# A two-problem attention decode: the framework's context closed behind the first six loads, the rest a bare program

## The chip, the cores and the metric

One core of one Trainium2 chip. The metric is device time in microseconds (us) of one execution, taken as the median of several runs. The engines are named as in the profile: PE is the matrix engine, DVE the vector engine, ACT the scalar engine, POOL is GpSimd, SP the engine that here only issues transfers. A "q" behind a name (SPq, ACTq) means the queue of that engine, on which transfers are issued.

## The reference: what is computed

Two attention layers decode one token each, A over a whole cache and B over its last 4096 positions. Both have 32 heads of width 128, each with its own keys and values, all bf16. The outputs of 512 each are set side by side.

```python
q = (x @ wq).reshape(1, 1, 32, 128)              # x: 1x1x512, wq: 512x4096
scores = einsum("bhqd,bhkd->bhqk", q, k) * 128 ** -0.5
p = softmax(scores)                              # A: 16384 keys a head; B: the last 4096
o = einsum("bhqk,bhkd->bhqd", p, v)
y = o.reshape(1, 1, 4096) @ wo                   # wo: 4096x512
# result: concatenate([yA, yB], axis=-1)
```

The caches that must be read are 32 x 16384 x 128 x 2 bytes x 2 for A and a quarter of it for B. With the weights that is 352 MB.

## The kernel before

**Stages.** The work is 20 steps of 8 MB of keys and 8 MB of values. Steps 0, 7, 13 and 19 are B steps (eight heads each), the other 16 are A steps (two heads each). Three 8 MB slots hold the data: `slotX` and `slotY` take the keys of even and odd steps, `slotV` takes the values of every step but the last, whose values go into `slotX`.

**One step.** DVE multiplies the keys by the query in place (L300, two halves), adds the 128 products of a key in a tree (L309, then the reduction of L316 into `sc`), and takes a maximum (L323). PE transposes the maxima (L389), DVE makes one maximum of a head and copies it to all partitions' places in `Mr` (L331, L335), PE transposes that back (L391), and ACT copies it times -1/sqrt(128) into `bias` (L347), takes the exponential (L352) and spreads the probabilities into `pm` (L360). PE multiplies them with the values in 64 small matmuls (L396) into `o`, ACT copies `o` to `osb` (L383), and PE folds it into the accumulators of A and B with two matmuls whose weights `fwA` and `fwB` choose the rows (L406). ACT writes the fold weights of a step at L376 or L379. Where step T-1 belongs to the other layer, ACT first clears the old weights (L374). There are six such places: T = 1, 7, 8, 13, 14, 19.

**What orders the work.** All waits are written by hand with counting semaphores. `_Lane.need` makes an engine wait for a token, `_Lane.did` makes one, and `_Loads.put` makes a token of a transfer. PE runs 19 of the 20 steps in a loop (L456) and takes tickets (L164). SP issues every load in program order: keys of step T+1 when DVE has reduced step T-1 (L316), values of step T when PE has used those of step T-1 (L396). POOL waits for the values of a step and passes this on to PE as a ticket (`to_v`, L431). In the last step SP issues the six loads of the two output weights `wo` (L441), once PE has used the values of step 18.

**Start.** ACT issues the two loads of x (L205). SP issues four loads of 4 MB: `wq` of B (L196), the first half of B's keys (L180), `wq` of A (L196), the second half (L180). Beside them POOL makes an identity (L213, L215) and clears `fwA`, `fwB` and part of `PA` (L220). DVE clears two buffers (L227), makes masks and patterns (L229 to L236), and, when PE has transposed x (L242), spreads it into block matrices (L246, L255). PE multiplies these with `wq` (L270), and ACT copies the queries (L276).

**End.** When the last piece of `wo` is there PE ends the output of B (L588), DVE copies it (L594), ACT and SP each store half (L598), and ACT waits for the stores (L602).

**The framework's part.** Buffers come from tile pools of a `TileContext` (opened at L628), and everything from L202 to L602 lies in one critical section of it (L201). The program that results has these parts around the hand-written one: after the start-up of L617 (four constants by POOL, one barrier over all engines) SP posts a semaphore at L201, on which all five engines wait and branch into the section; behind the section stand a chain of drains and semaphores that ends in one of SP (L201), and then a barrier, a clearing of the semaphores by POOL, and a second barrier (L628).

Of the kernel before, what the change touches and what calls it, by code (L numbers as in the profile page):

```python
# [8 lines left out]
F32 = mybir.dt.float32  # L9
BF16 = mybir.dt.bfloat16  # L10
P = 128
# [45 lines left out]
def kernel(  # L57
# [24 lines left out]
    low = ctx.enter_context(tc.tile_pool(name="low", bufs=1))  # L82
    slots = ctx.enter_context(tc.tile_pool(name="slots", bufs=1))
    high = ctx.enter_context(tc.tile_pool(name="high", bufs=1))
    banks = ctx.enter_context(tc.tile_pool(name="banks", bufs=1, space=bass.MemoryType.PSUM))

    def sbuf(pool, name, n, dt=F32, p=P):
        return pool.tile([p, n], dt, tag=name, name=name)

    def bank(name):  # L90
        return banks.tile([P, 512], F32, tag=name, name=name)

    qA = sbuf(low, "qA", HQ // 2 * DH, BF16)
    qB = sbuf(low, "qB", HQ // 4 * DH, BF16)
    identf = sbuf(low, "identf", P)
    fw = [sbuf(low, "fwA", P), sbuf(high, "fwB", P)]
    Mr = sbuf(low, "Mr", P, p=2)
    PB = sbuf(low, "PB", QR)
    PA = sbuf(low, "PA", 16)
    csA, csB = sbuf(low, "csA", HQ // 2), sbuf(low, "csB", HQ // 4)  # L100
    maskA, maskB = sbuf(low, "maskA", 2), sbuf(low, "maskB", 4)
    sbuf(low, "pad", 8)
    X, Y, W = (slots.tile([P, 2 * CH, DH], BF16, tag=n, name=n) for n in ("slotX", "slotY", "slotV"))
    pm = sbuf(high, "pm", 2 * CH // 4 * QR + QR, BF16)
    osb = sbuf(high, "osb", 512)
    sc = sbuf(high, "sc", 2 * CH)
    m, M, bias = sbuf(high, "m", 2), sbuf(high, "M", 4, p=2), sbuf(high, "bias", 2)
# [33 lines left out]
    for T in range(HQ // 2 + HQ // 8):  # L141
# [8 lines left out]

    pe, dve, act, pool, sp = (
        _Lane(e, tc.alloc_semaphore(n))
# [5 lines left out]
    in_x, in_wqB, in_wqA, in_v, in_out = (_Loads(tc.alloc_semaphore(n)) for n in ("in_x", "in_wqB", "in_wqA", "in_v", "in_out"))  # L158
    in_k = [[_Loads(tc.alloc_semaphore(f"in_k{a}{b}")) for b in range(2)] for a in range(2)]
    in_last = [_Loads(tc.alloc_semaphore(f"in_last{u}")) for u in range(2)]  # L160
    to_m, to_r, to_pm, to_v, to_f = (tc.alloc_semaphore(n) for n in ("to_m", "to_r", "to_pm", "to_v", "to_f"))
# [12 lines left out]
    def load(T, cache_a, cache_b, dst, loads, parts=(0, 1)):  # L174
        s, g = steps[T]
        if s is A:
            return [loads[0].put(nc.sync.dma_start(out=dst, in_=a_pair(cache_a, g)))]
        n = CH * DH
        return [
            loads[u].put(nc.sync.dma_start(out=dst[:, u * n : (u + 1) * n], in_=b_window(cache_b, 2 * g + u)))  # L180
            for u in parts
        ]
# [11 lines left out]
    def load_wq(s, dst, loads):  # L194
        return loads.put(
            nc.sync.dma_start(  # L196
                out=dst.rearrange("p (c f) -> p c f", c=KC), in_=s.wq.rearrange("(p c) f -> p c f", c=KC)
            )
        )

    with tc.tile_critical(no_gpsimd_drain=True):  # L201
        half = CH * DH  # L202
        xrow = pm[0:2, 0:D]
        for s in (B, A):
            x_in = in_x.put(nc.scalar.dma_start(out=xrow[s.k : s.k + 1, :], in_=s.x[0, :, :]))  # L205
        wq = [fW[:, half : 2 * half], fW[:, 0:half]]
        wq_in = [None, load_wq(B, wq[1], in_wqB)]
        load_k(0, (0,))
        wq_in[0] = load_wq(A, wq[0], in_wqA)
        load_k(0, (1,))  # L210


        t = pool.did(nc.gpsimd.memset(identf[:, :], 0.0))  # L213
        pool.need(t)
        ident = pool.did(nc.gpsimd.affine_select(  # L215
            out=identf[:, :], in_=identf[:, :], compare_op=ALU.not_equal, fill=1.0, base=0,
            pattern=[[-1, P]], channel_multiplier=1,
        ))
        for f in (fw[0][:, :], fw[1][:, :], PA[:, 0:8]):
            cleared = pool.did(nc.gpsimd.memset(f, 0.0))  # L220
        n = KC * P
        xb = [osb[:, :].bitcast(BF16)[:, 0 : 2 * n], fY[:, 0 : 4 * n]]
        two_b = fY[0:2, 8 * n : 8 * n + 2]
        xT = [fY[:, 8 * n + 64 * (k + 1) : 8 * n + 64 * (k + 1) + KC] for k in range(2)]
        for s in (B, A):
            s.xb = xb[s.k].rearrange("p (h c m) -> p h c m", h=s.nh, c=KC)
            dve.did(nc.vector.memset(xb[s.k], 0.0))  # L227
        dve.need(ident)
        two = dve.did(nc.vector.tensor_copy(two_b, identf[0:2, 0:2]))  # L229
        for s in (B, A):  # L230
            dve.did(nc.vector.tensor_reduce(out=s.mask[:, :], in_=by_head(s, identf[:, :]), axis=AX.X, op=ALU.add))
        t = dve.did(nc.vector.tensor_reduce(
            out=PB[:, :], in_=identf[:, :].rearrange("p (g x) -> p x g", g=NG), axis=AX.X, op=ALU.add
        ))
        dve.need(t)
        consts = dve.did(nc.vector.tensor_tensor(out=PA[:, 8:16], in0=PB[:, 0:8], in1=PB[:, 16:24], op=ALU.add))  # L236

        xps = wide[:, 0 : 2 * KC].rearrange("p (c s) -> p c s", s=2)
        pe.need(x_in, two)
        xr = xrow.rearrange("s (p c) -> s c p", c=KC)  # L240
        for c in range(KC):
            mm = nc.tensor.matmul(xps[:, c, :], lhsT=xr[:, c, :], rhs=two_b, start=True, stop=True)  # L242
        turned = pe.did(mm)
        dve.need(turned)
        for s in (B, A):
            t = dve.did(nc.vector.tensor_copy(xT[s.k], xps[:, :, s.k]))  # L246
        dve.need(t)
        for s in (B, A):
            for j in range(s.nh):
                dst = s.xb[:, j, :, :]  # L250
                if s is A:
                    dst = dst.rearrange("p c (h i) -> p c h i", h=s.nh)[:, :, j, :]
                else:
                    dst = dst.rearrange("p c (i h) -> p c i h", h=s.nh)[:, :, :, j]
                t = dve.did(nc.vector.tensor_copy(dst, xT[s.k].unsqueeze(2).broadcast_to([P, KC, P // s.nh])))  # L255
            s.spread = t
        pool.need(turned)
        zeroed = pool.did(nc.gpsimd.memset(pm[:, :], 0.0))

        qcopy = []  # L260
        for s in (B, A):
            pe.need(wq_in[s.k], s.spread)
            w = wq[s.k].rearrange("p (c g h d) -> p c h g d", c=KC, h=s.nh, d=DH)
            for g in range(0, HQ // s.nh, 4):
                qp = (t0, t1)[len(qcopy) % 2][:, :].rearrange("p (g d) -> p g d", d=DH)
                if len(qcopy) >= 2:
                    pe.need(qcopy[-2])
                for k in range(KC * s.nh):
                    c, j = divmod(k, s.nh)
                    mm = nc.tensor.matmul(  # L270
                        qp, lhsT=s.xb[:, j, c, :], rhs=w[:, c, j, g : g + 4, :],
                        start=(k == 0), stop=(k == KC * s.nh - 1),
                    )
                projected = pe.did(mm)
                act.need(projected)
                qcopy.append(act.did(nc.scalar.copy(s.q[:, g : g + 4, :], qp)))  # L276
                s.q_in = qcopy[-1]
            if s is B:
                freed_y = projected
                pe.need(zeroed)  # L280
                for a in (accA, accB):
                    mm = nc.tensor.matmul(
                        a[:, :], lhsT=pm[:, 0:P], rhs=pm[:, 0:512], start=True, stop=False, skip_group_check=True
                    )
                seeded = pe.did(mm)
        freed_w = projected
        loop0 = pe.n
        TR1, TR2, PV, FOLD = 1, 2, 3, 4

        def at(T, k):  # L290
            return (pe.sem, loop0 + 4 * T + k)
# [3 lines left out]
        def scores_prod(T, u):  # L295
            s, g = steps[T]
            kt = kflat(T)[:, u * half : (u + 1) * half].rearrange("p (l d) -> p l d", d=DH)
            j = g if s is A else 2 * g + u
            dve.need(kin[T][min(u, len(kin[T]) - 1)], s.q_in)
            return dve.did(nc.vector.tensor_tensor(  # L300
                out=kt, in0=kt, in1=s.q[:, j : j + 1, :].broadcast_to([P, CH, DH]), op=ALU.mult
            ))

        def scores_tree(T, lo, hi, t):
            k = kflat(T).rearrange("p (l d) -> p l d", d=DH)[:, lo:hi, :]
            w = DH // 2
# [7 lines left out]
            if T >= 1:  # L314
                dve.need(exped[T - 1])
# [317 lines left out]
```

## Time and profile before

| what | value |
|---|---|
| median of 3 runs | 822.28 us (822.17 to 822.59) |
| the profiled execution's own time | 822.12 us |
| its span, first to last instruction | 820.2 us |
| DVE busy | 755.9 us (92%) |
| PE busy | 193.7 us (24%) |
| ACT busy | 58.1 us (7%) |
| POOL busy | 2.9 us, 10 instructions |
| bytes read | 352.32 MB, 430 GB/s over the span |

Times inside the execution count from the span's first instruction. The profiled execution took 1.9 us more than its span, and 0.16 us less than the median. Drains, branches and semaphore instructions do not count as busy and have no row of their own on the page; the trace holds a start and a duration for each, and some of these are quoted by number.

### The profile page before, as it was taken

The numbers are of one execution on the slowest core, as the hardware profiler recorded it, in microseconds if no ns is written. First come the engines' busy times: TensorE is split into PE (matmuls) and PEld (weight loads), VectorE is DVE, ScalarE is ACT, GpSimd is POOL, SyncE is SP. The second block draws the span as 40 slices with busy tenths as digits, with TensorE's granted clock in tenths as the row PEclk, the third lists the DMA queues.
The fourth block names the chain that finished last, engine by engine and source line by source line (L and its number), as shares of the span: only waits on it lengthen the run. The fifth ranks groups of instructions, "written<-read, shape, count | busy, mean of one in ns | idle before, by whom it ended". The sixth has DMA issues, their size and how long they took to land. (4 is left out here: it accounts for less than half of the span.)

```text
span 820.2 us, 4069 instructions
## 1 busy us (share of the span) xinstructions
PE 193.7 (24%) x1638; PEld 78.4 (10%) x1638; DVE 755.9 (92%) x264; ACT 58.1 (7%) x171; POOL 2.9 (0%) x10
## 2 busy tenths in 40 slices
PE   3500312223030403030403122130304030304036
PEld 1200100101010101010101001010101010101012
DVE  2899999999999999899999999998999999999992
ACT  0101000001010000100000000010100000000010
POOL 1000000000000000000000000000000000000000
PEclk9865656565665656565656565655656565656568
DMA  9999999999999999999999999999999999999997
GB/s 384 435 434 436 457 412 454 416 454 416 454 416 451 411 449 428 420 446 431 438 422 447 422 447 414 455 413 431 438 454 416 454 416 454 416 431 438 431 435 312
DMA packets 8084, 352.40 MB, mean 430 GB/s; under 512 B 907, under 2 KB 1038, under 8 KB 1294
## 3 DMA queue, kind: packets, MB, share of 16 engines
q1 hardware_dynamic: 8068, 352.33, 99.3%
q8 instruction: 3, 0.05, 0.0%
q14 instruction: 3, 0.02, 0.0%
q10 hardware_dynamic: 10, 0.00, 0.0%
HBM read 352.32 MB, written 0.00 MB: 430 GB/s over the span
## 5 line engine op out<-in xcount | busy, mean ns | idle before, releaser
L309 DVE TENSOR_TENSOR slotY<-slotY 128x8192 bf16<-128x8192 bf16 (+4 forms) x52 | 168.2, 3234 | 1.7
L300 DVE TENSOR_TENSOR slotX<-slotX,qA 128x16384 bf16<-128x16384 bf16 x18 | 156.3, 8682 | 14.0 <-DMA slotX<-in_A_k_cache_dram 14.0
L309 DVE TENSOR_TENSOR slotX<-slotX 128x8192 bf16<-128x8192 bf16 (+4 forms) x44 | 167.0, 3795 | 1.5
L396 PE MATMUL o<-slotV,pm 128*32 128x512 bf16 x1216 | 111.9, 548 | 193.8 <-PEq L164 193.8
L300 DVE TENSOR_TENSOR slotY<-slotY,qA 128x16384 bf16<-128x16384 bf16 x14 | 121.6, 8682 | 9.4 <-DMA slotY<-in_A_k_cache_dram 9.4
L396 PEld LDWEIGHTS o<-slotV,pm 128*32 128x32 bf16 x1216 | 46.5, 132 | 251.5 <-issue 245.4
L389 PE MATMUL sm<-identf,m 128*2 128x128 f32 x20 | 7.4, 372 | 195.6 <-PEq L164 195.6
L300 DVE TENSOR_TENSOR slotY<-slotY,qB 128x16384 bf16<-128x16384 bf16 x6 | 52.1, 8682 | 0.0
L391 PE MATMUL sm<-identf,Mr 2*128 2x2 f32 x20 | 4.7, 234 | 190.5 <-PEq L164 190.5
L347 ACT ACTIVATE bias<-sm 128x1 f32<-128x1 f32 (+1 forms) x20 | 3.4, 171 | 438.2 <-PE sm L391 438.2
L383 ACT COPY osb<-o 128x512 f32<-128x512 f32 x20 | 11.7, 585 | 273.1 <-PE o L396 273.1
L300 DVE TENSOR_TENSOR slotX<-slotX,qB 128x16384 bf16<-128x16384 bf16 x2 | 17.4, 8692 | 13.4 <-ACT qB L276 13.4
L406 PE MATMUL accA<-osb,fwA 128*128 128x512 f32 x38 | 20.8, 630 | 14.8 <-PEq L164 14.8
L316 DVE TENSOR_REDUCE sc<-slotY 128x256 f32<-128x2048 bf16 (+1 forms) x13 | 23.3, 1794 | 0.4
L316 DVE TENSOR_REDUCE sc<-slotX 128x256 f32<-128x2048 bf16 (+1 forms) x11 | 23.0, 2092 | 0.4
L391 PEld LDWEIGHTS sm<-identf,Mr 2*128 2x128 f32 x20 | 3.5, 177 | 196.3 <-issue 196.3
L389 PEld LDWEIGHTS sm<-identf,m 128*2 128x2 f32 x20 | 1.6, 81 | 211.2 <-issue 211.2
L406 PE MATMUL accB<-osb,fwB 128*128 128x512 f32 x40 | 20.5, 594 | 0.5 <-PEq L164 0.5
L360 ACT ACTIVATE pm<-osb,maskA 128x256 bf16<-128x256 bf16 x32 | 14.5, 501 | 0.5
L352 ACT ACTIVATE osb<-sc,bias 128x256 bf16<-128x256 f32 (+1 forms) x24 | 11.3, 471 | 0.6
L270 PE MATMUL t<-slotV,slotY 128*128 128x512 bf16 x32 | 9.5, 471 | 5.9 <-DMA slotV<-in_B_wq_dram 5.9
L270 PE MATMUL t<-slotV,osb 128*128 128x512 bf16 x32 | 8.4, 430 | 9.3 <-DMA slotV<-in_A_wq_dram 9.3
(72 smaller groups left out, 98.2 us busy)
## 6 DMA issues: line engine op xcount, KB each, us to landing
slotV<-in_B_v_cache_dram SPq DMA_DIRECT2D x6, 4096.0 KB, 31.6
slotY<-in_B_k_cache_dram SPq DMA_DIRECT2D x6, 4096.0 KB, 35.3
slotX<-in_B_k_cache_dram SPq DMA_DIRECT2D x2, 4096.0 KB, 30.5
slotX<-in_B_v_cache_dram SPq DMA_DIRECT2D x2, 4096.0 KB, 35.3
slotV<-in_B_wq_dram SPq DMA_DIRECT2D x1, 4096.0 KB, 12.3
slotV<-in_A_wq_dram SPq DMA_DIRECT2D x1, 4096.0 KB, 30.4
slotV<-in_A_wo_dram SPq DMA_DIRECT2D x1, 4096.0 KB, 23.2
slotV<-in_B_wo_dram SPq DMA_DIRECT2D x1, 2048.0 KB, 27.5
```

The source lines that it names most:

```text
L270: mm = nc.tensor.matmul(qp, lhsT=s.xb[:, j, c, :], rhs=w[:, c, j, g : g + 4, :], start=(k == 0), stop=(k == KC * s.nh - 1),)
L300: return dve.did(nc.vector.tensor_tensor(out=kt, in0=kt, in1=s.q[:, j : j + 1, :].broadcast_to([P, CH, DH]), op=ALU.mult))
L309: t = dve.did(nc.vector.tensor_tensor(out=k[:, :, 0:w], in0=k[:, :, 0:w], in1=k[:, :, w : 2 * w], op=ALU.add))
L316: kfree[T] = dve.did(nc.vector.tensor_reduce(out=sc[:, lo:hi], in_=k[:, :, 0:8], axis=AX.X, op=ALU.add))
L347: t = act.did(nc.scalar.activation(out=bias[:, 0:U], in_=sm[:, P : P + U], func=ACT.Copy, scale=-inv))
L352: exped[T] = act.did(nc.scalar.activation(out=p[:, u * n : (u + 1) * n], in_=sc[:, u * n : (u + 1) * n], func=ACT.Exp, scale=inv, bias=bia ...
L360: mm = nc.scalar.activation(out=by_chunk[j], in_=p.rearrange("p (u i c) -> p u i c", u=2, c=4), func=ACT.Copy, scale=s.mask[:, j : j + 1],)
L383: nc.scalar.copy(osb[:, :], o[:, :]).then_inc(to_f, 1)
L389: pe.did(nc.tensor.transpose(sm[0:2, 0:P], m[:, 0:2], identf[:, :]))
L391: pe.did(nc.tensor.transpose(sm[:, P : P + 2], Mr[0:2, :], identf[0:2, 0:2]))
L396: mm = nc.tensor.matmul(o[r0 : r0 + QR, :], lhsT=pm[:, QR * i : QR * (i + 1)], rhs=vf[:, 512 * i : 512 * (i + 1)], start=(i < NG), stop=(i ...
L406: mm = nc.tensor.matmul(a[:, :], lhsT=fw[k][:, :], rhs=osb[:, :], start=False, stop=len(sides) == 1, skip_group_check=True,)
```

## The change

Four things change; the work between them keeps its order.

- The pools are gone. Buffers are taken with plain allocations, in the order of the list, so that `fwB` (512 bytes a partition) now lies ahead of the three slots and not behind them.
- The six first loads are issued inside the context, each named as an instruction that the framework gives no semaphore of its own (`early`). Then the context is closed and compiled (`tc.close()`, `tc.compile()`), which puts its end there: all that follows stands behind it, and there is no critical section. Semaphores come from the program itself. At the end POOL, in place of ACT, waits for the stores and clears all semaphores; nothing follows.
- The factor -1/sqrt(128) moves from ACT's copy into `bias` (L347) to DVE's copy into `Mr` (L335), which becomes a multiplication by a scalar.
- ACT's clearing of old fold weights (L374) goes. For T = 1, 7, 8, 13, 14 POOL does it with a memset, when PE has done the fold of step T-1 and ahead of its wait for the values of step T. The one at T = 19 is left out.

The lines that stood in the critical section move out by one level; this is not shown.

```diff
-    def sbuf(pool, name, n, dt=F32, p=P):
-        return pool.tile([p, n], dt, tag=name, name=name)
+    def sbuf(name, n, dt=F32, p=P):
+        return nc.alloc_sbuf_tensor(name, [p, n], dt)
...
-    fw = [sbuf(low, "fwA", P), sbuf(high, "fwB", P)]
+    fw = [sbuf("fwA", P), sbuf("fwB", P)]
...
+    sems = []
+    def semaphore(name):
+        sems.append(nc.alloc_semaphore(name))
+        return sems[-1]
...
+    def early(inst):
+        tc.no_tile_sem_insts.add(inst.ins.name)
+        return inst
...
-    with tc.tile_critical(no_gpsimd_drain=True):
     for s in (B, A):
-        x_in = in_x.put(nc.scalar.dma_start(out=xrow[s.k : s.k + 1, :], in_=s.x[0, :, :]))
+        x_in = in_x.put(early(nc.scalar.dma_start(out=xrow[s.k : s.k + 1, :], in_=s.x[0, :, :])))
     wq = [fW[:, half : 2 * half], fW[:, 0:half]]
     wq_in = [None, load_wq(B, wq[1], in_wqB)]
     load_k(0, (0,))
     wq_in[0] = load_wq(A, wq[0], in_wqA)
     load_k(0, (1,))
+    tc.close()
+    tc.compile()
...
-            nc.vector.tensor_copy(
-                by_head(s, Mr[0:U, :]), M[0:U, 0 : s.nh].unsqueeze(2).broadcast_to([U, s.nh, P // s.nh])
+        nc.vector.tensor_scalar(
+            out=by_head(s, Mr[0:U, :]), in0=M[0:U, 0 : s.nh].unsqueeze(2).broadcast_to([U, s.nh, P // s.nh]),
+            scalar1=-inv, scalar2=None, op0=ALU.mult,
             ).then_inc(to_r, 1)
...
-            t = act.did(nc.scalar.activation(out=bias[:, 0:U], in_=sm[:, P : P + U], func=ACT.Copy, scale=-inv))
+        t = act.did(nc.scalar.activation(out=bias[:, 0:U], in_=sm[:, P : P + U], func=ACT.Copy))
...
-                was, h = steps[T - 1]
-                if was is not s:
-                    n = 4 * was.nh * was.units
-                    old = fw[was.k][:, n * h : n * (h + 1)]
-                    act.did(nc.scalar.activation(out=old, in_=PB[:, 0:n], func=ACT.Copy, scale=0.0))
...
             vin[T] = load(T, A_v_cache, B_v_cache, fW, (in_v, in_v))
+            if T >= 1 and steps[T - 1][0] is not steps[T][0]:
+                was, h = steps[T - 1]
+                n = 4 * was.nh * was.units
+                pool.need(at(T - 1, FOLD))
+                pool.need(pool.did(nc.gpsimd.memset(fw[was.k][:, n * h : n * (h + 1)], 0.0)))
             pool.need(vin[T][-1])
             nc.gpsimd.sem_inc(to_v, 1)
...
-        act.need(stored)
+    pool.need(stored)
+    nc.clear_and_free_semaphores(sems)
```

## The prediction

> **What bounds the kernel now.** I read the page first, then the chain of waits, then the start in order of time, then the waits of DVE and SP.
>
> ```profile
> span 820.2 us, 4069 instructions
> ...
> DMA  9999999999999999999999999999999999999997
> ...
> q1 hardware_dynamic: 8068, 352.33, 99.3%
> ```
>
> The DMA row is nine tenths or more in all slices but the last, and SP's queue accounts for 99.3% of what 16 DMA engines could give in the span. In the trace the first packet of this queue starts at 2.0 us and the last one of `wo` ends at 816.6; in between some 16 packets are always in flight. 352.3 MB in 814.6 us is 432.5 GB/s.
>
> ```profile
> 785.97 30.65 DMA slotV<-in_B_wo_dram
> 816.62 0.04 issue
> 816.66 0.66 PE last L588 x16
> 817.32 0.02 issue
> 817.35 0.29 DVE slotY L594
> ```
>
> The chain that ended last (start, duration, what) is a transfer up to 816.6, and then one matmul group and one copy. So the span has three parts: **a head** of 2.0 us until data flows, **the stream** of 814.6 us, **a tail** of 3.6 us.
>
> ```profile
> DVE slotX L300 <- DMA slotX<-in_A_k_cache_dram: 14.0, 9, 2.6
> DVE slotX L300 <- ACT qB L276: 13.4, 1, 13.4
> DVE slotY L300 <- DMA slotY<-in_A_k_cache_dram: 9.4, 7, 1.4
> ```
>
> DVE, 92% busy, waits for keys in 16 steps, 23.4 us together (waits: total, times, longest): some 1.5 us a step. It is second, close behind the stream. An edit can change the time by moving the start of the stream, by letting it run dry, by changing its rate, or in the tail.
>
> **The head.** The profile's start in order of time:
>
> ```profile
> 0.95 0.42 SPq L196 DMA_DIRECT2D slotV<-in_B_wq_dram  x1
> ...
> 1.44 0.63 SPq L180 DMA_DIRECT2D slotX<-in_B_k_cache_dram  x1
> ...
> 2.73 0.55 SPq L180 DMA_DIRECT2D slotX<-in_B_k_cache_dram  x1
> ...
> 7.06 0.20 PEld L242 LDWEIGHTS wide<-slotY,pm 2*128 2x128 bf16 x4 [7.06 <-DMA pm<-in_A_x_dram]
> ...
> 7.42 1.83 POOL L258 MEMSET pm<- 128x2080 bf16 x1 [5.41 <-PE wide L242]
> 7.66 2.18 DVE L255 COPY slotY<-slotY 128x128 bf16<-128x128 bf16 x4
> 9.65 0.50 DVE L255 COPY osb<-slotY 128x256 bf16<-128x256 bf16 x2
> 13.26 6.95 PE L270 MATMUL t<-slotV,slotY 128*128 128x512 bf16 x20 [5.90 <-DMA slotV<-in_B_wq_dram]
> ```
>
> By the trace SP passes the start-up barrier at 0.652, posts the section's semaphore at 0.720, branches at 0.795 and issues at 0.952. Post and wait go. If the branch goes as well, the issue follows the barrier in 0.07 us, as the post did: 0.23 us earlier. If a branch stays, it comes at 0.72 and the issue 0.157 behind it as now: 0.08 earlier. I take the middle, **-0.15 us**, and it counts in full, since the stream behind it has no gap.
>
> What the close adds stands behind SP's last early issue, which ends at 3.28 (2.735 + 0.546), say 3.15. The framework's end now takes, from SP's arrival at 819.349 to the release at 820.14, 0.79 us: two barriers and a clear. All engines then start the setup at about 3.3 (one barrier, no clear) to 4.1; POOL started at 0.94, so by 3.2 us later at most. Cover: DVE's work ahead of PE's transposition of x ran from 1.23 to 2.69, at +3.2 to 5.9, and x is there only at 7.06. DVE's last pattern (L236, ends 3.65) comes to 6.85. So the transposition isn't moved at all. Were it moved, a second cover follows: the block matrices are ready at 10.14, `wq` of B at 13.25, 3.1 us later. Cost **0**, beyond both covers its full size in the queries' time, but not yet in the stream: the first four loads hold 16.8 MB, 38.8 us, until 40.8; the next load, now issued at 22.8, could be issued as late as 39.7 (first packet 1.04 after the issue, as at the start).
>
> **The middle.** POOL's five memsets: the nearest rows are 0.10 us (128x8, L220) and 0.20 (128x128). At T = 1 the fold ends at 90.7 and the values land at 120.6 (POOL's ticket): 30 us of cover, and it's alike in the others, since the load of values is issued as PE ends its matmuls, 2.7 us before the fold ends. Cost **0**; without that cover 0.2 us each plus a semaphore. ACT loses six clears of 0.2 us; behind them it waits 14 us for PE (L383), in the tail 5.85: **0**. `Mr` as a scalar multiplication: now 0.21 to 0.27 us as a copy; the nearest TENSOR_SCALAR (L514, 128x4) takes 0.23. So 0.06 either way, 20 times, in DVE's 1.5 us a step; `bias` without a factor keeps its 0.17 (fixed cost of one column). **0**. In the last step, 0.06 lies on the way to PE's output of B, which starts at 812.17 and then still waits for pieces of `wo` three times (1.28, 0.59, 0.51 us). The same wait hides it.
>
> Here a row speaks against the change: DVE's first two copies at L255 took 1.75 us each by the trace, the next two of the same shape 0.33, and the slow ones ended within 0.2 us of POOL's memset (7.42 to 9.25). POOL's memset can hold up DVE. At 0.2 us five times that is 1.0 us of DVE at most, in steps of which each has 1.5 to spare. The other way round POOL waits for one DVE instruction, 8.7 us at the longest, under 30 of cover. The Trainium skill ("SBUF — State Buffer", "Who interferes with whom") states an exclusive lock on a port pair shared by the two, which copies can take, while a two-input tensor_tensor isn't blocked by a GpSimd instruction that only writes. By that rule the tree would not notice and DVE's part of the sum is 0; by the row alone it is 1.0 us, which would show in the time (822.1) only where DVE had no wait left. No run here shows a memset beside the tree.
>
> The slots move by 512 bytes. No run here shows another address; 814.6 us hang on it, with either sign. I take 0.
>
> **The tail.** SP's store is issued at 817.67. ACT sees all stores at 818.979. Then, by the trace, come a drain and a post (819.135 to 819.29), the barrier (819.35 to 819.52), POOL's drain (819.541) and clear (819.668, 0.222 long, to 819.89), the second barrier (to 820.185). Afterwards POOL sees the stores at about 818.98 and has its drain and clear left: 0.127 to the clear and 0.222: 819.33. That saves 820.185 - 819.33 = 0.86 us. Bounds: without the drain 0.98; with a second clear, where the semaphores aren't one range, 0.6; with a barrier that the compiler still puts at the end, 0.2 to 0.6. I take **-0.85 us**, nearest to the rows of the clear itself.
>
> **The sum**: 822.12 - 0.15 - 0.85 = 821.1 for the profiled execution; the median of the runs lies 0.16 above it, so some 821.3, and I forecast **821.2 us**. That is 0.13% less. About 0.2%, 1.6 us, is what a measurement of this kernel can tell from no change.
>
> **The rivals.**
> - *More is saved at the end* (12%). 1.9 us of the execution lie outside the span. If the other engines' share of that now runs beside POOL's wait, up to half of it goes too, and 820.3 results. For it: four engines are through 1 us earlier. Against: POOL is last either way. The Trainium skill ("Runtime: NRT & Kernel Launch", "The ~15µs preamble/postamble breakdown") puts a barrier over all engines right behind the kernel; by that rule nothing runs beside POOL's wait and this rival falls back to the forecast. No run here shows what lies outside the span.
> - *The end stays* (10%): the close leaves a barrier behind at the program's end. Only the head's 0.15 and a little remain: 822.0.
> - *The close waits for the loads ahead of it* (5%), the case on the slower side. Decisive is whether SP's drain, or a semaphore of the framework, waits for open transfers. Then the setup begins at 40.8. Its chain takes 5 us (identity to block matrices), and 9.6 us pass from the first projection matmul (13.25) to the next key load (22.83): issue at 55.4, first packet at 56.4, and the stream stands dry for 15.6 us: 837. It costs nothing until the setup is delayed by the covers named above. Against it: SP's drain at 818.127 took 0.1 us while its own store was still under way until 818.98.
> - *Another rate at the new addresses* (5%, 3% slower, 2% faster): half a per cent is 4 us, 817 or 825. It decides from 2.4 ns in a 32 KB packet of 1.22 us.
> - *Code that isn't there in time* (6%): parts of the program lie in other places, and a fetch could hold up an engine. In the stream it's covered by DVE's 1.5 us and the queue's depth; ahead of the last matmuls a microsecond or two would show in full: 822 to 824, half of it over 0.2%.
>
> My own forecast holds the remaining 62%, 820.7 to 821.7.
>
> **The numbers.** Range 820.2 to 822.6: it holds the forecast, the first two rivals and the smaller half of the last, and leaves out some 13%. Faster by over 0.2% (under 820.6): the first rival and the faster addresses, with a little of my forecast, 15%. Slower by over 0.2% (over 823.9): the waiting close 5, addresses 3, code 3: 11%. Within: 74%.
>
> **What would show it.** Head: SP's first issue at 0.72 to 0.88, with no L201 ahead of it; the setup's first POOL and DVE instructions at 3.3 to 4.1; PE's L242 still waiting for x near 7; L270 still waiting for `wq` of B near 13.1. Middle: POOL's five memsets well ahead of the tickets; DVE's rows within 0.1 us of now; a DMA row of nines. Tail: the chain still ending in `wo`, L588, L594, with one clear by POOL behind the stores and a span of about 819.2. I am wrong if L270 waits for DVE, if the DMA row has a gap, if 32 KB packets take another time, or if the difference between time and span is no longer 1.9.

## The result, and the profile after

The changed kernel takes 820.97 us (median of 20 runs, 820.70 to 821.29). The kernel before, run beside it, takes 822.49 us (20 runs, 822.12 to 822.77). The ratio is 0.9982 with a 95% interval of 0.9975 to 0.9989: 1.5 us less. The interval lies below 1, so the gain is told from noise, and it is a little under the 0.2% that were named as the bound. The forecast was 821.2.

The page of the kernel after, its span, the DMA row and SP's queue:

```profile
span 819.2 us, 4049 instructions
...
DMA  9999999999999999999999999999999999999998
...
q1 hardware_dynamic: 8068, 352.33, 99.5%
```

The span is 1.0 us shorter and the DMA row as full as it was. The chain that ended last (start, duration, what) ends in the same way:

```profile
786.30 30.19 DMA slotV<-in_B_wo_dram
816.50 0.04 issue
816.54 0.66 PE last L595 x14
817.20 0.02 issue
817.23 0.29 DVE slotY L601
```

Before, the matmuls behind the last transfer began at 816.66, now at 816.54. So 0.12 us of the gain lie ahead of this point and 0.90 behind it. The first packet starts 0.22 us earlier (1.78 in place of 2.00), but in this pair of executions the stream took 0.11 us more (814.73 in place of 814.62); in the kernels below whose setup isn't held back for all four loads it took 814.51 to 814.84. The start of the kernel after, in order of time:

```profile
0.74 0.41 SPq L197 DMA_DIRECT2D slotV<-in_B_wq_dram  x1
...
2.50 0.55 SPq L181 DMA_DIRECT2D slotX<-in_B_k_cache_dram  x1
4.09 0.20 POOL L219 MEMSET identf<- 128x128 f32 x1 [3.65 <-POOLq L216]
...
4.38 0.91 DVE L233 MEMSET slotY<- 128x1024 uint32 x1 [4.38 <-PEq L216]
...
7.80 0.20 PEld L248 LDWEIGHTS wide<-slotY,pm 2*128 2x128 bf16 x4 [7.80 <-DMA pm<-in_A_x_dram]
...
8.40 2.18 DVE L261 COPY slotY<-slotY 128x128 bf16<-128x128 bf16 x4
10.38 0.50 DVE L261 COPY osb<-slotY 128x256 bf16<-128x256 bf16 x2
13.10 1.46 PE L276 MATMUL t<-slotV,slotY 128*128 128x512 bf16 x3 [5.01 <-DMA slotV<-in_B_wq_dram]
```

SP issues 0.215 us earlier (0.737 in place of 0.952). POOL and DVE start 3.15 us later, behind the close (L216). The first projection still waits for its weights and not for DVE: it begins at 13.10 in place of 13.26.

By the trace the end is this: POOL sees the stores at 818.857, its drain takes 0.100, the clear runs from 818.986 for 0.182, and nothing follows. From the stores to the last instruction it is 0.31 us; before it was 1.21.

### The profile page after: what moved, and what is told of

Its sections match the earlier page's. It is cut to its first block, busy times and chain, and to the rows that moved or that the text cites. A ratio compares the mean times of both kernels' runs of the same rounds, so it can differ in the third digit from the quotient of the medians.

```text
span 819.2 us, 4049 instructions
## 1 busy us (share of the span) xinstructions
PE 191.5 (23%) x1638; PEld 78.0 (10%) x1638; DVE 755.7 (92%) x264; ACT 57.5 (7%) x165; POOL 3.5 (0%) x15
## 5 line engine op out<-in xcount | busy, mean ns | idle before, releaser
L398 PE MATMUL o<-slotV,pm 128*32 128x512 bf16 x1216 | 107.9, 533 | 193.8 <-PEq L165 193.8
L359 ACT ACTIVATE osb<-sc,bias 128x256 bf16<-128x256 f32 (+1 forms) x24 | 11.3, 470 | 0.6
```

What stands on the lines that cost most here:

```text
L359: exped[T] = act.did(nc.scalar.activation(out=p[:, u * n : (u + 1) * n], in_=sc[:, u * n : (u + 1) * n], func=ACT.Exp, scale=inv, bias=bia ...
L398: mm = nc.tensor.matmul(o[r0 : r0 + QR, :], lhsT=pm[:, QR * i : QR * (i + 1)], rhs=vf[:, 512 * i : 512 * (i + 1)], start=(i < NG), stop=(i ...
```

## The experiments

Every kernel was timed against the kernel before on the same chip (822.59 us on the chip of the first four, 822.44 on that of the second four, 822.50 on that of the last four). "Outside" is the time of an execution less its span, the median over the executions of a kernel.

| kernel | us | less the kernel before | span, median | outside |
|---|---|---|---|---|
| before (three chips) | 822.59, 822.44, 822.50 | | 820.2 to 820.3 | 2.32, 2.24, 2.33 |
| control | 820.91 | -1.68 | 819.0 | 1.87 |
| old_end | 821.46 | -1.13 | 819.6 | 1.81 |
| loads_behind_close | 821.56 | -1.03 | 819.7 | 1.87 |
| old_addresses | 821.04 | -1.55 | 819.1 | 1.87 |
| no_context | 820.98 | -1.46 | 819.1 | 1.89 |
| setup_waits_wqB | 820.90 | -1.54 | 819.0 | 1.87 |
| setup_waits_all | 837.18 | +14.74 | 835.3 | 1.89 |
| act_clears | 821.12 | -1.32 | 819.1 | 2.02 |
| act_extra6 | 821.12 | -1.38 | 819.1 | 2.08 |
| act_extra60 | 820.95 | -1.55 | 819.0 | 1.91 |
| factor_on_act | 820.98 | -1.52 | 819.0 | 1.88 |
| act_as_before | 821.51 | -0.99 | 819.3 | 2.22 |

The theory at the outset was the prediction's sum, with the sizes of the traces: the stream starts 0.22 us earlier, the end is 0.90 shorter, all else is hidden. That makes 1.1 us, and the medians show 1.5. The rivals were what could hold the other 0.4: a faster stream at the new addresses, or something outside the span.

**control.** The changed kernel again.

> The changed kernel again, unaltered, as the yardstick for the others. My theory (the sum of the head, 0.22 us by the trace, and the end, 0.90): 1.1 us under the kernel before. Rivals that find 0.4 us more somewhere (a stream that runs faster, or time outside the span): 1.5 under it. The time less the span, execution by execution, tells the last from the others: 1.9 in both kernels by my theory, less here by the rival of the end.

The interval of its ratio, 0.9970 to 0.9988, covers both sums. The executions one by one settle where the rest is: the spans differ by 1.2 to 1.3 us, and outside it is 1.87 (1.81 to 1.96) against 2.32 (1.89 to 2.49). Some 0.4 us of the gain lie outside the span. The profiled execution of the kernel before had 1.93 there, one of the lowest of that kernel, which hid this.

**old_end.** The two barriers are put back.

```diff
     pool.need(stored)
+    nc.all_engine_barrier()
     nc.clear_and_free_semaphores(sems)
+    nc.all_engine_barrier()
```

> A barrier over all engines is put back ahead of the clearing of the semaphores, and one behind it. My theory: 0.5 us more than the control, all of it inside the span, behind the stores, as the two barriers of the kernel before took (0.2 and 0.3). The rival that the other engines' end runs beside POOL's wait: 0.5 in the span and up to 0.4 outside of it. If the end costs nothing: no difference.

The time is 0.55 us longer than the control's, and the span 0.6. By the trace the first barrier takes from 818.87 to 819.08, and the second ends the span at 819.71, 0.29 behind the clear (819.233 and 0.182). Outside it is 1.81, not more. So the end works as costed, and the rival that the other engines' end runs beside POOL's wait falls: here all five end together, and nothing grows outside.

**loads_behind_close.** The close comes ahead of the six loads.

```diff
-        tc.no_tile_sem_insts.add(inst.ins.name)
...
+    tc.close()
+    tc.compile()
     half = CH * DH
...
     load_k(0, (1,))
-    tc.close()
-    tc.compile()
```

> The context is closed ahead of the six first loads and not behind them. My theory: the first load is issued at some 1.3 us in place of 0.74, and the whole 0.6 us show in the time, since the stream has no gap. If DVE set the pace behind the start, or the stream caught up: no difference.

The first load is issued at 1.380, 0.64 later than in the control, and the time is 0.65 longer. The stream took 814.78 us there and 814.75 in the control. A shift of its start counts in full.

**old_addresses.** `fwB` is allocated behind the slots.

```diff
-    fw = [sbuf("fwA", P), sbuf("fwB", P)]
+    fwA = sbuf("fwA", P)
...
+    fw = [fwA, sbuf("fwB", P)]
     pm = sbuf("pm", 2 * CH // 4 * QR + QR, BF16)
```

> The fold weights of B are allocated behind the three slots again, so that the slots lie 512 bytes lower, as before the change. My theory: no difference from the control (0.1 us at most). The rival of the addresses: the stream is longer by some 0.4 us, and 32 KB packets take longer by about 0.6 ns on average.

The median is 0.13 us over the control's, with ranges that overlap (820.77 to 821.29 and 820.68 to 821.13). The stream of the profiled execution took 814.68 us, 0.07 less than the control's. A 32 KB packet took 1217.8 ns on average against 1217.0, the sign that the rival wants, but the kernels at the new addresses spread from 1216.7 (act_extra6) to 1218.0 (loads_behind_close), and the median span is 819.1 against 819.0. There is no sign of the 0.4 us; 0.1 can't be excluded.

**no_context.** The kernel runs without any context.

```diff
-        tc.no_tile_sem_insts.add(inst.ins.name)
...
-    tc.close()
-    tc.compile()
...
-    with _tile.TileContext(nc) as tc:
+    class _Bare:
+        pass
+    tc = _Bare()
+    tc.nc = nc
+    if True:
```

> No framework context at all: nothing to close, so the setup starts right behind the start-up barrier, 3.1 us earlier than in the control. My theory: the close is hidden by the wait for the first weights, so no difference from the control (0.1 us at most). If the close cost anything, this kernel is faster by that much, at most 3 us.

It takes 820.98 us, within 0.1 of the changed kernel (820.97), of the control, and of setup_waits_wqB on the same chip (820.90). POOL starts at 0.73 in place of 4.09, and the first load is issued at 0.730, as in the control. So the close of the context costs nothing, to 0.1 us, where it stands.

**setup_waits_wqB** and **setup_waits_all.** How much cover is there, and what lies beyond it?

```diff
     tc.compile()
+    pool.need(wq_in[1])
+    dve.need(wq_in[1])
```

> POOL and DVE begin the setup only when the first 4 MB of weights have landed (13.1 us). By my theory the queries come some 5 us later (first projection at 18 in place of 13.1) and the next key load is issued at 28 in place of 23, but the stream holds data until 40.6: no difference in the time. If DVE, which is 92% busy, sets the pace once it has been delayed: up to 5 us more.

```diff
     tc.compile()
+    for e in (pool, dve):
+        e.need(wq_in[1], wq_in[0], *kin[0])
```

> POOL and DVE begin the setup only when all four first loads have landed: what the change would cost if its close waited for the loads ahead of it. My theory: the setup begins at about 40.8, the next key load is issued 15 us behind that, the stream stands dry for 15.6 us, and the time is that much longer: 836.6. If DVE's 1.5 us a step were eaten up instead and it set the pace: between 830 and 850, without the gap in the DMA row being the whole difference.

With 9 us of delay (POOL from 4.09 to 13.09) the time is 820.90. The start, and the waits of DVE (total, times, longest), of this kernel:

```profile
13.09 0.20 POOL L221 MEMSET identf<- 128x128 f32 x1 [12.65 <-DMA slotV<-in_B_wq_dram]
...
17.82 9.30 PE L278 MATMUL t<-slotV,slotY 128*128 128x512 bf16 x32 [2.63 <-DVE osb L263]
27.16 0.33 SPq L178 DMA_DIRECT2D slotY<-in_A_k_cache_dram  x1
...
27.86 8.69 DVE L308 TENSOR_TENSOR slotX<-slotX,qB 128x16384 bf16<-128x16384 bf16 x1 [9.87 <-ACT qB L284]
```

```profile
DVE slotX L308 <- DMA slotX<-in_A_k_cache_dram: 12.5, 8, 2.3
...
DVE slotY L308 <- DMA slotY<-in_A_k_cache_dram: 6.9, 5, 1.4
```

The first projection waits for DVE now and is 4.7 us late, DVE's first multiplication 4.0 us (23.82 in the kernel after), and the next key load is issued at 27.16. In the kernel after the waits were these:

```profile
DVE slotX L306 <- DMA slotX<-in_A_k_cache_dram: 15.1, 9, 2.6
...
DVE slotY L306 <- DMA slotY<-in_A_k_cache_dram: 8.2, 6, 1.4
```

Together they are 3.9 us shorter here: DVE makes up for its late start out of its waits, and the time doesn't change.

With 38 us of delay it is 16.3 us more than that (837.18). The same view, and then each engine's busy time by stretch (stretch and its length, PE, PEld, DVE, ACT, POOL, granted clock, DMA share, GB/s):

```profile
42.15 0.20 POOL L221 MEMSET identf<- 128x128 f32 x1 [41.71 <-DMA slotX<-in_B_k_cache_dram]
...
55.54 0.33 SPq L178 DMA_DIRECT2D slotY<-in_A_k_cache_dram  x1
```

```profile
0.00:40.00 40.00, 0.00 (x0) 0.00 (x0) 0.00 (x0) 1.28 (x1) 0.20 (x4) 1.00 0.96 410
40.00:41.00 1.00, 0.00 (x0) 0.00 (x0) 0.00 (x0) 0.00 (x0) 0.00 (x0) 1.00 0.91 393
41.00:57.00 16.00, 10.37 (x44) 4.54 (x45) 5.40 (x16) 1.17 (x2) 2.66 (x6) 1.00 0.17 57
```

From 41 to 57 us the DMA share is 0.17. The stream is dry from 41.75 to 56.49 (14.7 us) and thins out ahead of it; first packet to last it takes 830.95 us in place of 814.75, so 16.2 of the 16.3 us are the gap and the thin stretch ahead of it. This is the price of the third rival (15.6 was worked out), and DVE does not add to it.

**act_clears.** ACT clears old fold weights, POOL does not.

```diff
         if T >= 1:
             act.need(at(T - 1, FOLD))
+            was, h = steps[T - 1]
+            if was is not s:
+                n = 4 * was.nh * was.units
+                old = fw[was.k][:, n * h : n * (h + 1)]
+                act.did(nc.scalar.activation(out=old, in_=PB[:, 0:n], func=ACT.Copy, scale=0.0))
...
-                pool.need(at(T - 1, FOLD))
-                pool.need(pool.did(nc.gpsimd.memset(fw[was.k][:, n * h : n * (h + 1)], 0.0)))
```

> Old fold weights are cleared by ACT again (six times), not by POOL (five times). My theory: no difference from the control (0.1 us at most), since POOL's memsets have 30 us of cover and ACT waits behind its own. If POOL's memsets held up DVE and DVE set the pace, this kernel would be faster by up to 1 us.

The span is the control's (819.1 against 819.0), but outside it is 2.02 (1.95 to 2.11), which I had not expected. Here was a part of the missing 0.4 us. It had to come from ACT's six instructions more or from POOL's fewer. The last four kernels look for it.

**act_extra6** adds six idle instructions to ACT at the places of the clears, **act_extra60** sixty during the setup.

```diff
-    sbuf("pad", 8)
+    spare = sbuf("pad", 8)
...
+            if steps[T - 1][0] is not s:
+                act.did(nc.scalar.activation(out=spare[:, :], in_=PB[:, 0:8], func=ACT.Copy, scale=0.0))
```

```diff
+    spare = sbuf("spare", 60)
...
+    act.need(ident)
+    for i in range(60):
+        act.did(nc.scalar.activation(out=spare[:, i : i + 1], in_=identf[:, i : i + 1], func=ACT.Copy, scale=0.0))
```

> What is open: time less span is 2.2 to 2.3 us in the kernel before and 1.88 in the control, and 2.03 with ACT's clears back. Here POOL clears as in the control, and ACT does six idle writes of eight columns to a spare buffer at the places of its old clears. If ACT's own program (its number of instructions) makes the 0.15 us outside the span: 2.03 again. If POOL's fewer instructions made it: 1.88. The span is that of the control, 819.0, in either case.

> ACT does 60 idle one-column copies during the setup, where it waits anyway. If the time outside the span grows with the number of ACT's instructions (0.15 us for six): some 3.4 us, or a step of some other size. If only what ACT does late or POOL does counts: 1.88. The span is that of the control, 819.0.

With six, outside is 2.08 (1.94 to 2.12), though POOL clears as in the control: it is ACT's program, not POOL's. With sixty it is 1.91 (1.80 to 1.99), near the control: sixty in the setup do not make it grow, and the steady growth that I had put first is refuted. The other reading named there, that only what ACT does late counts, is left open by it.

**factor_on_act** puts the factor back, **act_as_before** that and the clears (as in act_clears, not shown again) and the wait for the stores.

```diff
-            scalar1=-inv, scalar2=None, op0=ALU.mult,
...
-        t = act.did(nc.scalar.activation(out=bias[:, 0:U], in_=sm[:, P : P + U], func=ACT.Copy))
+        t = act.did(nc.scalar.activation(out=bias[:, 0:U], in_=sm[:, P : P + U], func=ACT.Copy, scale=-inv))
...
-    pool.need(stored)
+    act.need(stored)
+    pool.need(act.did(nc.scalar.copy(osb[0:1, 0:1], osb[0:1, 0:1])))
```

> The factor -1/sqrt(128) is back in ACT's copy into bias, and DVE copies to Mr without it. My theory: no difference in the span (0.1 us at most) and none outside of it. If the 20 instructions with a factor on ACT make part of the 0.4 us outside the span: 2.0 to 2.2 there.

> ACT's part is as in the kernel before (clears, factor, and ACT that waits for the stores, with one small copy more to pass this on to POOL), in the bare program. If ACT's program makes the time outside the span: 2.2 to 2.3 us. If it is the framework's parts: 2.03, as with the clears alone. The span is 0.2 to 0.4 us longer than the control's by the copy between the stores and POOL's clearing.

The factor alone changes nothing (span 819.0, outside 1.88). With ACT's part as before, outside is 2.22 (2.12 to 2.30), near the 2.24 to 2.33 of the kernel before. So the 0.4 us come back with ACT's part, and they stayed away when the old end, the old addresses or the late loads were put back, or the context left out. Within ACT's part, the clears alone give 0.15; what the rest does without them was not run.

By ACT's records in the trace, the time outside is this: 172 of them (no_context) 1.89; 176 (control) 1.87; 180 (old_end) 1.81; 182 (act_clears, act_extra6) 2.02 and 2.08; 183 (act_as_before) 2.22; 185 (before) 2.24 to 2.33; 236 (act_extra60) 1.91. By number that is a hump, not a slope. But act_extra60 has its sixty in the setup, the clears and the six of act_extra6 stand in the steps, so number and place were changed together, and these runs don't tell them apart; the four records that ACT has more at the very end of old_end did not lengthen it. Nor is the size fixed by the program: of the 93 executions of the kernel before, 12 had 1.88 to 1.96 outside, like the changed kernel, and 81 had 2.03 to 2.49.

Why is open. No instruction is recorded outside the span, so it isn't known whether this time lies ahead of the first instruction or behind the last. The Trainium skill ("Runtime: NRT & Kernel Launch", "Instruction fetch mechanics") says that engines get their code in blocks of 256 instructions; a hump would fit a program whose end falls at an awkward place in a block. The traces, which do hold the packets of the instruction queues (q8 and q14), show no sign of it: all kernels have six or seven packets of 8 KB ahead of the first instruction (11.3 to 7.3 us before it) and none behind the last, and from 100 us on, control (1.85 us outside in the profiled execution), act_clears (2.07), act_extra6 (2.07) and act_as_before (2.16) have theirs at the same five places, within 0.4 us: 140, 194, 547, 805 and 815 us. So the fetch is argued and not shown.

## Why the prediction was right, point by point

- **The bound.** Right: the stream, with nothing to fill in the gaps but its start and its end. loads_behind_close moved the start by 0.64 us and the time by 0.65.
- **The head.** Right, a little small: 0.215 us in place of 0.15. Post, wait and branch all went, so it came near the far bound (0.23). That a shift of the first load counts in full is shown by loads_behind_close, not by this pair of profiles, whose streams differ by 0.11 us.
- **The close.** Right in its cost, 0, shown by no_context. SP's last early issue ended at 3.05, its drain took 0.375, the release came at 4.03 and POOL began at 4.09, inside the forecast 3.3 to 4.1; DVE began at 4.38, behind it by as much as it was behind POOL before (0.29). The step that failed is the first cover: "the transposition isn't moved at all". DVE was through in time (its last pattern ended at 6.8), but x itself came at 7.80 in place of 7.07. The close isn't the cause: without it PE's wait for x ended at 7.69 (no_context). The second cover took it: the block matrices are ready at 10.89, 2.2 us ahead of the weights.
- **The close does not wait for the loads.** SP's drain ended at 3.48, with 16.8 MB under way until beyond 40. The reason given (a drain that passed an open store) held, and setup_waits_all confirms the price.
- **The middle.** Right. POOL's five memsets, and the groups of `Mr` before (L335) and after (L341), by line, engine, operation, form and count, then busy time, mean ns, idle time:

```profile
L335 DVE COPY Mr<-M 1x128 f32<-1x128 f32 (+1 forms) x20 | 4.5, 226 | 0.7
```

```profile
L341 DVE TENSOR_SCALAR Mr<-M 1x128 f32<-1x128 f32 (+1 forms) x20 | 4.5, 226 | 0.7
L436 POOL MEMSET fwB<- 128x32 f32 x3 | 0.4, 125 | 155.1 <-PE accB L408 155.1
L436 POOL MEMSET fwA<- 128x8 f32 x2 | 0.2, 106 | 427.9 <-PE accB L408 427.9
```

  The multiplication costs what the copy did. The memset at T = 1 runs at 88.83, and its ticket goes out at 120.7, when the values land: 32 us of cover. For the other four it is 29 to 30 us.
- **Row and rule on POOL's memset.** The Trainium skill ("SBUF — State Buffer", "Who interferes with whom") was right for the tree: the tree instruction that ran beside the memset at 88.83 (start 88.01) took 4.424 us, as the same one a step later without a memset beside it (4.424). The other four memsets also ran beside such an instruction, which took 4.424 to 4.425, against 4.424 to 4.426 for those without a memset. DVE's copies beside the long memset still took 1.75 us each, four instructions in 2.18 us, as before. So the five memsets cost DVE nothing, where the row alone gave up to 1.0 us.
- **The tail.** Right: 0.90 us in place of 0.85. There is one drain and one clear, as costed from the rows of the kernel before.
- **The time outside the span.** Here the working failed. I took it as 1.9 us in both kernels from a single execution; its median was 2.24 to 2.33 before and is 1.87 to 1.89 now. The sign named for it (a difference no longer 1.9) could not show this, since it is the kernel before that has more than 1.9. The rival "more is saved at the end" had the right place, but its mechanism fell with old_end, and its size, up to half of 1.9, was too large. The spans alone give 1.1 to 1.3 us by their medians, 1.0 by the two profiled executions; with 0.4 outside, that is the 1.5 to 1.7 us measured. About 0.4 us of the gain was thus not in the sum, and the forecast came within 0.3 us of the time because this term is small, not because it was foreseen.
- **The remaining rivals.** The end did not stay, the old addresses made 0.13 us, within the ranges, and no late code shows in the span: the chain that ends last has the same pieces as before.

## What to carry to other kernels

Where a stream of transfers fills the whole run, an edit that leaves the stream's rate alone and doesn't let it run dry counts only at the two ends: what stands ahead of the first load counts in full, and so do barriers behind the last store, while 9 us more ahead of the setup cost nothing here, since the queue still held data. Move a framework's closing work to a place where a transfer covers it, and work out the cover in us before doing it. For gains of a microsecond, compare the spans and the times of many executions, not those of one profiled run.

## What the runs showed of the hardware that was not expected

- Six instructions more on ACT in the steps, off every path, lengthened the time outside the span by 0.15 to 0.2 us, and sixty in the setup did not.
- The second of two loads of 1 KB on ACT's queue, beside the stream on SP's, got its packet 3.97 us behind its issue in the one trace of the kernel before (1.46 to 5.43) and 4.77 to 5.10 behind it in all changed kernels. In the kernel after it was issued 0.17 us earlier and came at 6.18, and PE's wait for x ended 0.73 us later. The cause is open. An earlier start of the stream isn't it: in loads_behind_close SP's first load is issued 0.43 us later than before, and the packet comes 5.05 behind its issue. Nor is the order of the first packets: in the kernel after, x's came behind SP's (2.17 against 1.78), in the control ahead of it (1.64 against 1.77), and the second came at 6.18 and 6.09.
- DVE, 92% busy, took a start of its first multiplication that was 4.0 us later (27.86 in setup_waits_wqB, 23.82 in the kernel after) without a change in the time.
